# Query products and their sums for four positions in one buffer, V products for two, logits as position, offset, head

## The chip, the cores and the metric

The kernel runs on one core of a Trainium2 chip. The metric is device time in microseconds (us) of one execution. Five engines work side by side, each on its own queue in order: PE (TensorE, matmuls), DVE (VectorE), ACT (ScalarE), POOL (GpSimd) and SP (SyncE, which here only issues DMAs). ACT and POOL issue DMAs too.

## The reference

Two mixers over the same input x (2048 positions, 640 columns) and a gate between them. A is a local attention: 32 heads of 20 columns, each position looks at 8 keys, those 0, 2, ..., 14 positions back. B is a filter in the frequency domain.

```
qkv = (x @ wqkv).reshape(B, S, 3, H, Dh)          # H = 32, Dh = 20
idx = pos[:, None] - 2 * arange(8)[None, :]        # 8 offsets, masked where negative
logits = einsum("bhsd,bhswd->bhsw", q, kg) * Dh ** -0.5
attn = softmax(logits, -1)
o = einsum("bhsw,bhswd->bhsd", attn, vg)
a = o @ wo
b = irfft2(rfft2(x) * (w_r + 1j * w_i))
g = sigmoid((x * gate_w).sum(-1, keepdims=True))
out = g * a + (1 - g) * b
```

## The kernel before

Position 16 p + j lies in partition p as row j, so a partition holds 16 neighbouring positions; even and odd j never meet in the attention and are worked on apart (`par` 0 and 1, 8 rows each). The work falls into stages on PE: `qkv` (x times wqkv as three matmuls of rounded parts; the results leave through ACT into a DRAM scratch), `freq` (16 groups g, each a small pipeline over PE, ACT, POOL and DVE: `u`, `v` on PE, `ab` on DVE, `x`, `z` on PE, `P` on POOL, `s` on DVE, `g` on PE) together with `project_even` (attention output of even rows times wo), `spatial` (the inverse transform over columns) and `project_odd`.

The attention itself uses no matmul. `attend` does it for one `par` and a group h of four heads (80 columns); there are 16 such calls, called units here and named 0a, 0b, 1a, ... 7b. A unit loads q, k and v rows from the scratch. Then, for pairs of positions jj, it multiplies q with the eight k rows (product `pr`) and sums it over the 20 columns of each head into the logits `L` (a `TENSOR_REDUCE` on DVE). Both are 1280 elements a partition long. DVE makes the product with q copied to PSUM (`qbank`) by ACT; in ten of the units (table `POOL_PR`) the last pair's product is POOL's, straight from SBUF. After the masks (ACT) come the largest logit per position and head `m` (DVE), the subtraction (POOL), the exponential (ACT), the sum `s` and its reciprocal (DVE), the scaling (POOL), and for each pair the V products `pv` (POOL, one instruction for each position) and their sum over the offsets, `o` (DVE).

The order on every engine is fixed: `Plan.record` writes each operation into a list, `Plan.order` permutes the list by a table of numbers (`ORDER`), and `Plan.issue` issues it in that order. All instructions therefore carry one line (L385 in the profile), and are told apart by their tiles.

Of the kernel before, what the change touches and what calls it, by code (L numbers as in the profile page):

```python
# [208 lines left out]
HQ(%xOkCb5Ti|9M&74oX@)~%FC+g&Um>cIj7Th&a$THElCM_Qxh94S8@_R$YuH^AlZ29A62|gtX_GwKt861v*&%|Lj%A~%)Ju4ard*J9-%@(h(=zcz=9{hy8`{2ylZ=~+70?!1ipBf(&
zwb}8-f;L(FVHcuzwYP7?2%s*U{nv&ECs$KBfw^t@z;C&Xf&zSgn_WXO0Ra-A{p=`KSTo&WCxLcHX{frWWSucqtk!hm#2nHJeX5P<a5rX;@Kti_Yl8ko7HnBP?BD0BCR!|nSp+9pO(On  # L210
7C*Q$o$wOs&SmSBdiC|DHG?D8$uS*E_ccd=5LY{i^BiXwbd{r0)D57<l%^E2DaY|53+8~ZxRJddAoRNdJYPz%5Lvh5W}S={Qu`$OJ}cwneg)RxR)(xpZMXtIs%DRMvJ7u?%%!@^1B8h@
(qlVz@tLYv`rnaOHo>WRfe{k*SBQiEnDF!z+o6MsFAJ=(MehAC+OQk;gfj{$D4Y9E8C&GfcpM}t1W|C%hJ#;L!7aan3ZqicP~xB7_Qnrj(tTe<@R?W&V{($jS4EF-5t#TOP0?OuT|3Qa
eIT(hT>jCQrecqER6AALUaUC?)=4v!RW)w9%$6TmkX}rmdZ1<A!<Ce0_LGFT-55A$ndz>!p$dHdxh1>o=3<(6z*KuxX86ZbhMDSB?~D@~6mK>u#>!XP<ORCokbE-Ovd^FevYd6|yTLNh
6LqbJKy?z;o)=#fxd)}q(t!E7s4(3|QOszQKMHHgt&?pyfYSMq-!@LPp=HMQOrhAsZ-JWy-C3Mc^Z`{5!$bngKocKj*>1lOfpe>gL<4DAk0)0!w_E-I8Ix5zA0pAPHAB79wZiA}lY^=h
Std;TST@mvK(Izv+y2xl{ZkLjAJfK%G&=WMvx-dxg6DMA424jO9cS?4TWJptst&`UzGq$ZfJ_rYlV4K31$NLXrgHytE*H`DST?S8Z+_yEBRpdjK2A~uXM4Nj32C4N!P4z2;Hqn$;QEkU
x#r;cod7g-0_+HHSjTx0G?wMOQFZ}koI>bLqzm3R1#oY}9`o)-A1NE;d6CRy2FU=-R;2owOP)Xp5@L{{lo`pBpk%V|R6g=MDVwD`bNH=OjT}S9%<^i$H2}^WSgi-blEMMxNCWOt@KVe#
HqSpv<!^C>%lNmv7RSF7$EOxNC{yKe#`U(Lx+?J!T>!ZP9DRYha-KfY6f?D)z+1)BTY#H0H8P_on~L7A?2-f-TVGlJ$NYiPg`Ivs?eZmoz*1s%9Xd;!3V#C-+$0Brl2%!N#H_A1i{L@S
P#-7P*l5}1Q+W5C%(=qlbU3pZ%otQHBXliSa7Eq92vyz1<`-h2wlnrTN(?T$K{1wyGNT3yESJ?d;(Zw=a_uas{jBg++Q~Nj2jh-_=z=SgoGX(xs<sgT2K8=TN&l`u^j-}yWbYSO(5cEw
hVcGl#lx!tpndKnI3W6}4nYMD+Pk`P27A{L32W`ao5f1Lx*Nb1X()n(JDUZ2O2az;7O<uub@cq%>A*E(_tL!Qq_R=1wNX@G<vau7PJDCp_$;h81hHJ;PIGy_$BYC9!FRj&Q%d@dloNT&
V}(@XS$iJK7_UBeT9exaHe0ZCd>(H!PSGFR8O~kQ=y2V-@rw&$Jg2mnKHs;xrCurTIvRujMxI%zzSsUAbNQyk@KBwL05WxN*Sm)5I2Xq^XZjzH)Ihl#)t51ss6A^!b?3)adQa(X1?V`Q  # L220
wEf(@vgv8sXd>1A(Inx$aDsF9o|pp|HZf+o&w(aEY-(nPPdJX2mvN>(E_fL#$UQPvI|Oa9cnbzr-e$^;-WQD_g83Pq)JF@6puq4=iw_oAzI4h0IpY+hbO=V@zz#KK7T>Y)df*No_7zw#
J`ZNS1m5yd>sTzrvwN&$9|njAQz>w>cl%q7wQZn?8p!=9m>5`9rRfIf_1}m*K9QWX2p$bk-U|1B1Z(^)NFjGTUi*=`v=?z{hl`I|qiO|ofbK~N2V}%VS*t!h=6?gk(z$O~7sEFHmYj%6
MNgL}676SI+-J!42{U}iie@2JyD7wX?tWyweu6+;9xiJSQlECBlw3cU6JNL9Qbq$0tUe_bx^QVlnRQ^tl#ei^!;Uy@((9<|ywE43$z4IgNR)3HBAWp^wA5G)i`pF3l<h}x3OgiJc*rTp
yDIhR4d;b1#P9;B=Fn!{JagvZWQ8Dna+>C8?PWN5+e!O%eKQFD7&UwCI9EJuzf24eM=px5vm)*=iSJQOsoOrV0(&B;X_MREg42C+90%XRnO_)k_RRKzcw`jk&FlJtxyJ@dT+yf~v((s8
-2h}>WX&Km>`JDrIZsB~HyMCyj)w7Emh<Bxtc+@vJ<-~GPXyd<K2@BwUFJSEEbOSLf-}5Tj30C4oH>gKhj@`yM0lgO1I|~8Uz5d)n(Ap~u7*R$VC*4V^uL@BrFYVSXJ!#;GPx$-`iB^*
2MiYfr5xOz@(Hn_ZO=uraJXL7TjCH2Oo22&4b<5GbESU)fMy@w<%JD=kBRvs^7YntD5lPeG0~#A(Y7f~=u1vSN3y;*%B)if3ZHyCNgsIjl_GRnl%27NSP+9t2PA;2H4bS5GyaV=>j*#x
*M~~EY1!7%?esLp+*GX}o-QD6C&^J6=;H8X|6(A(`yZi}Z}faaS0?Gjqv@lj&ep&tv$=yAF_CROwlnc;Gg~`p{^9llwa}e7zb`&fYr`LIz+M4&!D;pBW0~8c-9pQAVK~5|Lst>X_XHJf
BbHYtz@n{+NemE;D#YqvNyi@TUL%=x!c}A)W#~0YXI_9y%G_JmIy7up9F-wz0Ko(;nI?_m?Kd3a(}245c2v@Jf1OP32?$)b@4&S%LtI4Xl7SDnL8i5%lEDj)>G1TqOFDWr8uzjy&O3Nm
d$+wYoEer$Aq-KST1DqGF`N6nbu3i9J1y!73cVHXcW7RCc*0zmf=AnkP~}&rJ5)<G5jD!ivtsQGa!*YrUZ<x(O%YP2uxAQgki#<4cU6)m;~U+_$c%HUxDD2C>6*du+*nLhT21G%FSMTx
F9o90(I?=4__Uh>X7zl2S;|3%g?xk&&ZNy<yz%i{Sl87#;Hq(*dX#-S;0K7k`-=_DNmtn_cWizA<)OfVpjTP3DV~JDA&$35ndX-;RJ~3efGwiJ5Ht%!mBpiuzqzwAm%V<N$YT+%N<y?-  # L230
L$<-n`T;@{9ha=_DU5Caogirb*l5ll(=hVGvPaUVHGn@TTk@(O%Cg>+!F&Z>^a}MWs*HoAIXZ*IGmD&KQ1$s5UlW<f%b`0L6Zo}XxY*ejMiL6wZB3VWksk25LDcc$*m+|kO*MiA5qM!R
E4&I$iUB%e=t-&vI#oE3omS`8qhKNa{&xtjquCoj@gt~4hPP`#R?lah{_Fr2NG)2)6j`)6xWw-bn!#53kreFmg|f%8{Hi9hP;wz{AL5rvcI#V0DymT1c(Kucy<*0`8=s--Bri8zDH~#v
%-FB#M0Qq%ICg_IFP2C48|n56Sm9Um9k2fiPvpqah%)KEUW1~=uV*6=QB*z{Al8lvW9Q;ye=6Tp=v>L79H5IQ5X|z~#8hpnJr+Ga_QrkC4`Rhv7#WXovCK>ybSs8B6l~NOoIP)O5Fr!S
+}fcYgLx<p#v>wbK=gW?vhdCXZVtgKhsHNHj%~Qolp5+lQ(hjj51#p5_1_2~j|^=(cHJD!9j9&qpZdcxvk%!cXv8;;W{9m%oyJFbB38c|mac656_T8#{}Kg@00
# [732 lines left out]
```

## Time and profile before

| | |
|---|---|
| time, median of 3 runs | 453.96 us (453.48 to 454.35) |
| the profiled execution | 455.89 us, of which the span from the first to the last instruction is 454.1 us |
| PE busy | 441.2 us, 97% of the span |
| PE weight loads | 391.8 us, 86% |
| DVE busy | 409.8 us, 90% |
| POOL busy | 363.9 us, 80% |
| ACT busy | 211.9 us, 47% |

How to read it: PE is busy nearly all the time, so the time can only fall by what PE waits, and it rises when PE is made to wait more. DVE and POOL are second; where they stand still matters only if PE, or the end, waits for them. Busy times are unions, and the durations of neighbouring instructions on one engine overlap a little, so what an instruction costs a full engine is the distance from its start to the next one's.

### The profile page before, as it was taken

The page shows a single profiled execution, that of the slowest core. Times are in us where ns is not written, and L with a number is a line of the kernel's source. Part 1 is how long each engine was busy: PE and PEld are TensorE (multiplying, and loading weights), DVE is VectorE, ACT ScalarE, POOL GpSimd, SP SyncE. Part 2 cuts the span into 40 slices and gives each one's busy share as a digit, 9 for nine tenths or more (in the row PEclk, how much of TensorE's full clock was granted, in tenths as well). Part 3 has the DMA queues.
Part 4 walks back from the last instruction along what each step waited for, and adds up shares of the span by engine and source line. Part 5 has one row for each costly group of instructions (what it writes and reads, how often), then busy time and mean ns, then how long its engine had stood idle before and what let it go on. Part 6 is the DMA issues. An engine that isn't in the chain of part 4 may idle for free. (4 is left out here: it accounts for less than half of the span.)

```text
span 454.1 us, 7249 instructions
## 1 busy us (share of the span) xinstructions
PE 441.2 (97%) x2440; PEld 391.8 (86%) x2440; DVE 409.8 (90%) x519; ACT 211.9 (47%) x561; POOL 363.9 (80%) x316
## 2 busy tenths in 40 slices
PE   9999999999999999999998989999989999999996
PEld 6888888888889888899886769998877899999996
DVE  4899999899999999999978989999999997899484
ACT  4723165625226463255356666667554655342110
POOL 1158895899899898988977898976899998889810
PEclk9999999999999999999998999999999999999999
DMA  8998999887968979679979778989883331365932
GB/s 312 401 383 268 340 330 377 305 264 237 272 183 272 340 217 316 181 216 320 303 220 294 240 230 250 297 245 320 258 257 105 85 97 54 118 207 134 296 123 87
DMA packets 73956, 110.75 MB, mean 244 GB/s; under 512 B 21296, under 2 KB 50992, under 8 KB 73920
## 3 DMA queue, kind: packets, MB, share of 16 engines
q1 hardware_dynamic: 40192, 69.32, 46.8%
q10 hardware_dynamic: 32816, 36.97, 26.1%
q0 software_dynamic: 912, 4.00, 2.4%
q8 instruction: 19, 0.31, 0.3%
q14 instruction: 17, 0.14, 0.1%
HBM read 72.51 MB, written 32.84 MB: 232 GB/s over the span
## 5 line engine op out<-in xcount | busy, mean ns | idle before, releaser
L385 PE MATMUL qkv<-w,xo 128*128 128x480 f32 (+1 forms) x480 | 110.6, 385 | 0.0
L385 PE MATMUL qkv<-w,xe 128*128 128x480 f32 (+1 forms) x474 | 104.3, 382 | 0.0
L385 PEld LDWEIGHTS qkv<-w,xe 128*128 128x128 f32 x474 | 89.3, 189 | 15.2 <-ACT xe L385 0.9
L385 PEld LDWEIGHTS qkv<-w,xo 128*128 128x128 f32 x480 | 89.7, 189 | 13.8 <-ACT zg L385 0.2
L385 ACT COPY ev<-qkv 128x480 f32<-128x480 f32 x64 | 34.9, 558 | 48.3 <-PE qkv L385 35.9
L385 PE MATMUL woa<-wo,oT 128*128 128x320 f32 x240 | 47.2, 318 | 0.4 <-ACT oT L385 0.4
L385 PE MATMUL wob<-wo,oT 128*128 128x320 f32 x240 | 46.9, 315 | 0.2 <-ACT ya L385 0.2
L385 POOL TENSOR_TENSOR P<-P,wp 128x963 f32<-128x963 f32 (+1 forms) x16 | 35.4, 2212 | 6.6 <-DMA P<-X 4.0
L385 PEld LDWEIGHTS woa<-wo,oT 128*128 128x128 f32 x240 | 37.7, 188 | 1.1 <-ACT oT L385 0.6
L385 PEld LDWEIGHTS wob<-wo,oT 128*128 128x128 f32 x240 | 37.8, 188 | 0.6 <-ACT ya L385 0.4
L385 POOL TENSOR_TENSOR fx<-fx 128x160 f32<-128x160 f32 (+1 forms) x16 | 12.8, 818 | 24.2 <-DMA fc<-in_t_fc 17.1
L385 POOL TENSOR_TENSOR w<-raw,w 128x480 fp32r<-128x480 f32 (+1 forms) x20 | 24.8, 1262 | 5.3 <-ACT w L385 5.3
L385 ACT CAST oT<-oTp 128x384 fp32r<-128x384 f32 (+1 forms) x32 | 13.4, 427 | 30.9 <-PE oTp L385 17.3
L385 PEld LDWEIGHTS g<-mm,s 128*128 128x128 f32 x150 | 21.0, 190 | 7.1 <-ACT zg L385 5.0
L385 PE MATMUL g<-mm,s 128*128 128x128 f32 x150 | 23.5, 280 | 3.1 <-ACT zg L385 3.0
L385 DVE TENSOR_TENSOR oT<-oTp,oT 128x384 fp32r<-128x384 f32 (+1 forms) x32 | 15.2, 485 | 11.0 <-ACT oT L385 10.7
L385 PE MATMUL oa<-gt,zg 128*128 128x161 f32 (+1 forms) x96 | 24.0, 344 | 0.0
L385 PE MATMUL ob<-gt,zg 128*128 128x161 f32 (+1 forms) x96 | 22.0, 344 | 0.0
L385 PE MATMUL u<-bt,zc 128*128 128x240 f32 (+2 forms) x96 | 21.1, 335 | 0.7 <-DVE ab L385 0.7
L385 PE MATMUL v<-bt,zc 128*128 128x240 f32 (+2 forms) x96 | 21.5, 335 | 0.2
L385 DVE TENSOR_TENSOR fx<-fx 128x642 f32<-128x642 f32 (+2 forms) x24 | 19.2, 798 | 0.7
L385 PEld LDWEIGHTS u<-bt,zc 128*128 128x128 f32 x96 | 16.9, 199 | 2.9 <-PE g L385 0.9
(304 smaller groups left out, 1107.6 us busy)
## 6 DMA issues: line engine op xcount, KB each, us to landing
qkvd<-ev ACTq DMA_DIRECT2D x32, 480.0 KB, 4.8
wp<-in_ws SPq DMA_DIRECT2D x16, 642.0 KB, 5.9
raw<-in_wqkv SPq DMA_DIRECT2D x25, 240.0 KB, 5.9
fx<-in_x SPq DMA_DIRECT2D x8, 641.0 KB, 7.9
ot<-od SPq DMA_DIRECT2D x16, 320.0 KB, 3.9
P<-X ACTq DMA_DIRECT2D x30, 160.5 KB, 4.6
fd<-fx POOLq DMA_DIRECT2D x6, 640.0 KB, 5.6
f<-fd SPq DMA_DIRECT2D x6, 640.0 KB, 6.1
```

The costliest lines, as they stand in the source:

```text
L385: p.dve.memset(w, 0.0)
```

## The change

In `attend`, with `POOL_PR` as it was:

- The q copy, the product and its sum are made for four positions at once (2560 elements) where DVE makes them all, and for two where the last pair is POOL's. Of 54 products and 64 sums on DVE 32 and 42 are left, which is 22 fewer of each (the first four positions in all 16 units, the last four in the six units without a POOL product). The two `pr` buffers for two positions become one for four; the three places of `qbank` become one for four and one for two positions.
- The V products of two positions are one instruction: 64 instead of 128.
- The logits lie as position, offset, head (8, 8, 4) where they lay as position, head, offset (8, 4, 8). The sum of products now writes them without gaps. `m` and `s`, which reduce over the offsets, now read with a step of four elements (16 bytes) and took their eight offsets side by side before. The masks are written for the new layout.
- `ORDER` is a new table.

```diff
 ORDER = """
-T>t<81poj4|NsC0{{R31`zHT%QmDPk&^9H>y=H*?`Lk%9Gnl%)B_CdQV7rLsIrdLM6sJFoVB8Rk|2U=URH5DLwHy3}>N|I2375U5sNENOZ_r>p;QjNS0Qt^d&3_BFn1BL!{U(U9<aW#`
+T>t<81poj4|NsC0{{R31`zHT%QmDPk=#MDKuavHX(-*4-BtL4lZ(KsIOtW*vbH(DXn{6x>Y7x4d+OGq=Ut3x;+j-bV#DI*Cv$$xAC(TD;868c`#R9Own^O!b`yiAzYmH!y&eRc)d7yAj
...
-        self.qthird = [qb[:, GC * i : GC * i + GC] for i in range(3)]
-        self.qturn = -1
+        self.qplace = qb[:, 0 : 2 * GC], qb[:, 2 * GC : 3 * GC]
...
-        L = self.Lr.next(f"L{nm}", 8, 4, 8)
-        for jj in range(0, 8, 2):
-            pr = self.prr.next(f"pr{nm}{jj}", 2, 8, HC)
+        L = self.Lr.next(f"L{nm}", 8, 8, 4)
+        own = POOL_PR.get((par, h), ())
+        jj = 0
+        while jj < 8:
+            k = 2 if jj in own or jj % 4 or jj + 2 in own else 4
+            if jj % 4 == 0:
+                pair = self.one(f"pr{nm}{jj}", 4, 8, HC, tag="pr")
+            pr = pair[:, jj % 4 : jj % 4 + k]
             w = kt[:, jj : jj + 8]
-            w = bass.AP(tensor=w.tensor, offset=w.offset, ap=[w.ap[0], [HC, 2], [HC, 8], [1, HC]])
-            if jj in POOL_PR.get((par, h), ()):
-                mul, qj = G.tensor_mul, q[:, jj : jj + 2]
+            w = bass.AP(tensor=w.tensor, offset=w.offset, ap=[w.ap[0], [HC, k], [HC, 8], [1, HC]])
+            if jj in own:
+                mul, qj = G.tensor_mul, q[:, jj : jj + k]
             else:
-                self.qturn = (self.qturn + 1) % 3
-                mul, qj = V.tensor_mul, self.qthird[self.qturn]
-                A.copy(qj, q[:, jj : jj + 2].rearrange("p j c -> p (j c)"))
-                qj = qj.rearrange("p (j c) -> p j c", j=2)
-            mul(pr, w, qj.unsqueeze(2).broadcast_to([128, 2, 8, HC]))
+                mul, qj = V.tensor_mul, self.qplace[k == 2]
+                A.copy(qj, q[:, jj : jj + k].rearrange("p j c -> p (j c)"))
+                qj = qj.rearrange("p (j c) -> p j c", j=k)
+            mul(pr, w, qj.unsqueeze(2).broadcast_to([128, k, 8, HC]))
             V.tensor_reduce(
-                out=L[:, jj : jj + 2].rearrange("p j h r -> p j r h"),
+                out=L[:, jj : jj + k],
                 in_=pr.rearrange("p j r (h d) -> p j r h d", d=HD),
                 axis=AX.X,
                 op=ALU.add,
             )
+            jj += k
...
-        V.tensor_reduce(out=m, in_=L, axis=AX.X, op=ALU.max)
-        G.tensor_sub(L, L, m.unsqueeze(3).broadcast_to([128, 8, 4, 8]))
+        V.tensor_reduce(out=m, in_=L.rearrange("p j r h -> p j h r"), axis=AX.X, op=ALU.max)
+        G.tensor_sub(L, L, m.unsqueeze(2).broadcast_to([128, 8, 8, 4]))
         A.activation(out=L, in_=L, func=AF.Exp, scale=SCALE)
         s = self.sr.next(f"s{nm}", 8, 4)
-        V.tensor_reduce(out=s, in_=L, axis=AX.X, op=ALU.add)
+        V.tensor_reduce(out=s, in_=L.rearrange("p j r h -> p j h r"), axis=AX.X, op=ALU.add)
         V.reciprocal(s, s)
-        G.tensor_mul(L, L, s.unsqueeze(3).broadcast_to([128, 8, 4, 8]))
+        G.tensor_mul(L, L, s.unsqueeze(2).broadcast_to([128, 8, 8, 4]))
...
-            for i in range(2):
-                G.tensor_mul(
-                    pv[:, i].rearrange("p (h d) r -> p r h d", d=HD),
-                    vt[:, jj + i : jj + i + 8].rearrange("p r (h d) -> p r h d", d=HD),
-                    L[:, jj + i].rearrange("p h r -> p r h").unsqueeze(3).broadcast_to([128, 8, 4, HD]),
-                )
+            w = vt[:, jj : jj + 8]
+            w = bass.AP(tensor=w.tensor, offset=w.offset, ap=[w.ap[0], [HC, 2], [HC, 8], [1, HC]])
+            G.tensor_mul(
+                pv.rearrange("p j c r -> p j r c"),
+                w,
+                L[:, jj : jj + 2].rearrange("p j r h -> p (j r) h").unsqueeze(3).broadcast_to([128, 16, 4, HD]),
+            )
```

What the new table does is seen on the engines. DVE, where the attention begins (unit 0a: products, sums, then `m0a`), before:

```order
L385 TENSOR_TENSOR pr0a_344<-kt0a,qbank 128x1280
L385 TENSOR_REDUCE L0a<-pr0a_344 128x2x8x4
L385 TENSOR_TENSOR pr0a_345<-kt0a,qbank 128x1280
L385 TENSOR_REDUCE L0a<-pr0a_345 128x2x8x4
L385 TENSOR_TENSOR pr0a_346<-kt0a,qbank 128x1280
L385 TENSOR_REDUCE L0a<-pr0a_346 128x2x8x4
L385 TENSOR_TENSOR pr0a_347<-kt0a,qbank 128x1280
L385 TENSOR_REDUCE L0a<-pr0a_347 128x2x8x4
```

and after the change:

```order
L382 TENSOR_TENSOR pr0a_344<-kt0a,qbank 128x2560
L382 TENSOR_REDUCE L0a<-pr0a_344 128x128
L382 TENSOR_TENSOR pr0a_345<-kt0a,qbank 128x2560
L382 TENSOR_REDUCE L0a<-pr0a_345 128x128
L382 TENSOR_TENSOR pr0b_358<-kt0b,qbank 128x2560
L382 TENSOR_REDUCE L0b<-pr0b_358 128x128
L382 TENSOR_REDUCE m0a<-L0a 128x32
```

Eight instructions became four of twice the size, and `m0a` stands behind one long product and sum of the next unit, where it stood behind two short ones of each.

DVE, where the attention meets the first groups of `freq` (`ab1` and `ab2` are what PE needs for groups 1 and 2), before:

```order
L385 TENSOR_REDUCE o7a0_478<-pv7a0_479 128x160
L385 TENSOR_TENSOR pr6a0_504<-kt6a_500,qbank_63 128x1280
L385 TENSOR_REDUCE m7b_492<-L7b_487 128x32
L385 TENSOR_TENSOR ab1_606<-u1_605,vs1_604 128x321 x2
L385 TENSOR_REDUCE L6a_503<-pr6a0_504 128x2x8x4
L385 TENSOR_TENSOR pr6a4_506<-kt6a_500,qbank_63 128x1280
L385 TENSOR_REDUCE L6a_503<-pr6a6_507 128x2x8x4
L385 TENSOR_REDUCE o7a0_478<-pv7a2_480 128x160
L385 TENSOR_REDUCE L6a_503<-pr6a4_506 128x2x8x4
L385 TENSOR_TENSOR ab2_616<-u2_615,vs2_614 128x321 x2
```

and after:

```order
L382 TENSOR_TENSOR pr6a0_484<-kt6a_480,qbank_63 128x2560
L382 TENSOR_REDUCE o7a0_460<-pv7a0_461 128x160
L382 TENSOR_REDUCE L6a_483<-pr6a0_484 128x128
L382 TENSOR_TENSOR pr6a4_485<-kt6a_480,qbank_63 128x1280
L382 TENSOR_REDUCE m7b_472<-L7b_469 128x32
L382 TENSOR_TENSOR ab1_574<-u1_573,vs1_572 128x321 x2
L382 TENSOR_REDUCE o7a0_460<-pv7a2_462 128x160
L382 TENSOR_REDUCE L6a_483<-pr6a4_485 128x64 x2
L382 TENSOR_TENSOR pr6b0_498<-kt6b_494,qbank_63 128x2560
L382 TENSOR_TENSOR z1_577<-z1_577,wp1_569 128x321
L382 TENSOR_TENSOR ab2_584<-u2_583,vs2_582 128x321
```

One sum of 1280 elements (half of `L6a` from `pr6a0`) and the product `pr6a4` moved ahead of `ab1`; the long product of the next unit, `pr6b0`, moved ahead of `ab2`.

POOL, late in `freq` (`P13`, `P14` are products of the groups 13 and 14 that DVE, and then PE, wait for; `pv6b` are V products), before:

```order
L385 TENSOR_TENSOR pv6b2_528<-vt6b_517,L6b_519 128x8x80
L385 TENSOR_TENSOR P13_781<-P13_781,wp13_772 128x963
L385 TENSOR_TENSOR P13_781<-P13_781 128x321
L385 TENSOR_TENSOR pv6b2_528<-vt6b_517,L6b_519 128x8x80
L385 TENSOR_TENSOR pr5b6_555<-kt5b_548,q5b_550 128x1280
L385 TENSOR_TENSOR P14_794<-P14_794,wp14_785 128x963
```

and after:

```order
L382 TENSOR_TENSOR pv6b2_504<-vt6b_495,L6b_497 128x2x8x80
L382 TENSOR_TENSOR P13_749<-P13_749,wp13_740 128x963
L382 TENSOR_TENSOR P13_749<-P13_749 128x321
L382 TENSOR_TENSOR pr5b4_527<-kt5b_522,q5b_524 128x1280
L382 TENSOR_TENSOR P14_762<-P14_762,wp14_753 128x963
```

The two halves of a V product that stood on both sides of `P13` now stand ahead of it as one (`pr5b4` is the POOL half of the unit's second buffer, the product called `pr5b6` before).

More of the change, by code (lines that the diff above doesn't have):

```diff
@@ L209 @@
[L209 to L228, printed above, removed]
@@ L233 @@
-%-FB#M0Qq%ICg_IFP2C48|n56Sm9Um9k2fiPvpqah%)KEUW1~=uV*6=QB*z{Al8lvW9Q;ye=6Tp=v>L79H5IQ5X|z~#8hpnJr+Ga_QrkC4`Rhv7#WXovCK>ybSs8B6l~NOoIP)O5Fr!S
-+}fcYgLx<p#v>wbK=gW?vhdCXZVtgKhsHNHj%~Qolp5+lQ(hjj51#p5_1_2~j|^=(cHJD!9j9&qpZdcxvk%!cXv8;;W{9m%oyJFbB38c|mac656_T8#{}Kg@00
+T>t<81poj4|NsC0{{R31`zHT%QmDPk=#MDKuavHX(-*4-BtL4lZ(KsIOtW*vbH(DXn{6x>Y7x4d+OGq=Ut3x;+j-bV#DI*Cv$$xAC(TD;868c`#R9Own^O!b`yiAzYmH!y&eRc)d7yAj
+EI>SOMgyW|6IVlz?{etRp_rXb`FX*NuqcMI^kM|llCB(6G53>*B7=3~M0{u0Ya=^0f(PmqZ`fHQAq`b>c)G-m!{1GMkeO%3w5!`|y?wx@|1ewjdT@=Kl@C5@x#p3D<QH;VZ}5?8U3pvb
@@ new lines @@
+h@<J-B|+HRrQKW%$FZarh$91qAkyv5{G#RdK}ro(AV36-B_h$#Rl)Rw7bsS21{Xg{+35i~^m;jS5l$I}9A(gM<s8!?|5o47Y?^P*(xHMdCQ?Rgw~gB-vGf)t`k{C7Ja}(v?b`#_Fm7P2
+t@}HpL*34cKwpbI<F1*YmaRvz%o2B)WHSXDM1g~?Z*~dMYB-mKX@T+H35mNyq%3#OT-kd&;V-%KI|-SkW}c)8+0PjmVuu*~Y&yCqpvp7m;WM-vk@G%4V1=Qqo9h~~3Jny1*LkU~9jZM)
+=u%rc=2lu`#GwqxQivx`Pe6oMyJ=>B>C7=kMKJ@!Y$jlrcizcKL(7dW@Se-U2tr{}zjg>c`H_|Z%Ut-p-kX_6g!?Ab4J`u;qVDyW=>1PJ*{rafynC-e@b{l6<%URB3tab}Zj&eH-3$H)
+;Cl%1;!l937-H%NjIN${UMHH<>m&j!@gQHkW_l~r?5w^T1L*?bACdldu^QdNM52Gau2Bz#V?o{cP33@E@2apO{lAl14wbe=m<%+6VWwMd03=emuOc|U=?=1=V9L)^?G9ZK`IAA6@A+ua
@@ new lines @@
++~U2nZO;W(H1ZH(CGu-wUc#xcD`O3qce|Ncy-#_qFJ_U_U6zKk)eCzi7%+;Fw|l~7Kors>22p6bS1HPYux`|h6J{7F0?UokWVlCTUbujk&wcgAh`KsGjwGyiOt-C&UQmi4C&S%FzT+IS
+1NEPmi0Os>c1!C;&y)GfMP1igl#4EVGuq<H2bEdO#j|e0GEUpu`s4uizn1)Upnb_kKieIGFo<{|f`ld;_4RJRFI(s!<UGOg0St5`6gfk?(9tzgFf%`3DWye-{FXy>tQvS#K}##qV3r{%
+<gs&=SqJznEK5JJv|OyfXaTG-Ha}^Zu>j0=KAZt0#S|S0LYPY*s<frPzlwl?s1Z`+Rn7vrX39zzNI)B`(1!3W?2-qpn@XY{mcLDe#W-T&6jeAxY6<H|WMl_`3@o0lFYFg!hBFEBT_6FE
+^IW|~W4Az943N&i7^h0C+)Aw}<cb@1RSi_&2{2A#$0W$*j6&C$TGle=iLeY0y++xEWc3|&q*OP4HK`NAyVim5$cczUieCIZV(|9x_0C<{>r|-5;GGUryt<eE@3thNEq(<#C<IfU+NA0d
@@ new lines @@
+Hd=3#DmwFuN>)9u;!ri)^61tufHct+60}DlD>MZ}*G{i^+{!oBAu}=PjrkGRp8P)lbN3{J#AgLczXbvHU5-$(-^ST3+NPQt@6uCe$`|)NA#`IwQ3!DeDCLGJ*+9MADA@d1eTkMN`&ND>
+H<+L1rxNppJ2-W~3xKCkmuJ-y`&a=;c%L)eI>6t``+XYR*r4&jO$>Oy<~JZs3#%G>Qp2q~RF6Z=Raz#uhgw8I0_P@Em|s}`H~{DnhsHWuC_F>HYIcQ2>bFOwZ@I1GS5?<C^1+uJU>laf
++~EOqoH@hs9~Z+wWY2liGWt0MSgI@Br2jxN#UcwHT%z@q^|@0C>$PQ=j?2*9aT^E1ETwI0TJX~s#u|(GBN2C#Ov)4im_Bk;no=6?3duB0v$CFD3eg}`ZXoh*DS|%JA_)Xj#cd3)zQ%8~
+ZR?N^Ob`5aTFu3WHTlZzD)mooY74i$E#SZ*_$;5fzUiHujdGV~J6oYhN%6nF4VzY-13VSA(uHQLBHy<P5*uVl){FxDs084k`+q}920T&hR&iwcuBogMJQa5YC7Uv5Qg(6M{|<V`R01Nt
@@ new lines @@
+bC;-rx##B)r?)R+sIwLqm)Q_^AYF;|K%in326~LLI}%THhds4{lJ4nX(uPMjbH-I>q+VBG#GfE=o4v!q$pAeZ#!V8L&+Vi7)Ya}Su;|)_;U5yK#HHRdD(+c#Wj)51f^{wQ|FB|~Wije(
+<XrS(8UbWb{YaV&opfTE0VGXO-#E30bEcoWWG+Fz#xvm$BfEt21R|nU*IS_@WmYblICb4v$>WJ-`9*DoBAt9#34OBC!+W(Yc_eZ&vwo_?fWiuV>XIB$EeK(-=*d)`cvC-W?Z>>&9(Hw&
+vcZ8X<fke13gcr{>^Pc+{0zhu?TzAO+PRz9<+Fv>FrM(M3&w_JPNnBtw<n`4kr9d<8RhxgO)tndSA0=`$0gcKCT^k65Hab8-1X7)pqZPG{J$sbF4G{gc|`USVyx=e!@{L!z-!`#ld)IS
+UV`q>zXSuEWiu<3FG&<!BT-c47dq?y8txA!vFQoOF@r6#b+zI5g4g+y1lbSrd|n2)x0S&)$-;%1z-K0WX01G8rL1OfQW4r3R^@;1c1fVWbfZE7--4i*tr_Nn5kzRx@lI^V&$xV2_}MMu
@@ new lines @@
+_v5J=qvOUM5OielQ`p6)(q=d!_$-s=x3K!9saUXUN)e1zmO4w^;Shf~yA1eIRcGs_U68Z%L`DM2MVx;N%*ThdRT0IdwtbgnLl0DAt2e4wv4%W8+WnOE&+qj0i&7<><;V#w879sb6CiFm
+hKWbI&5tn)u*vD%!;mN52+#QAUuU)iI<SRFpm*T|U#mqog4piRzP=*Fryc9V$F`fv72oc}Ku2dp>_wuos#&5RxD^xTz1+A_pB{vRM34Z@I9ZOu{l}y}1RdyZiU({Fq~UtA8t<!ctM9r2
+8^53URH7UX0iA)L-~$ipR}Cpof(%rB<&(;-Cfg6Jeni~-)Nk(WV3{Coh&H#Glrst)6xDpr$1|)&h#5j9tbMjcJBf^IC}zs|a;;UHCVgxsnOB!xw#cGa`c!MGEYAV^&mk+g%D(oVuGP&O
+5*v9(4L4tCNKGHYNTk`2$z*Y-59=3}+g!Dyd+$`ia<g&`_IYg56)~-sqBt)^cCYDK7;Ur#8!HjpJ0BkmjYpV!1}#upkuLvG-x9?~gQv7Au3Z}^Ao5DmdpcKD86E8v$LM(-CASj=1$3@n
@@ new lines @@
+65B1x3hVH8UO|@yO`SAcBM^G|X4Z`%g!02JrZN5~P)jm*_(8aLyeqE=SdxlseVG>(=sfuW8AZ7CjDj#Kup7>xS;E-=Nmamw!tpb8E#d*N_j3LGOo;Lq<1^gcZZyE;*+Wh5p08QqUXo<Z
+L9JcsE0pH+m4PpayFtp;-P$RG;%$XG{sTqDU3nSaY{RB3pke*2k@I6Eq~yqviEs#$PG`W6ets7<#iexFpPGiv7v}$mZzkvsgXk1JVX%?U?yoFU{F}ZawDuD4+i#5>&FeqE%7sH~LYNBk
+sTWm>jE`R@9E%)hokhCOlk|nmx66!sW|!yY=tBr}HwO3;g+*-b;J{dr=9D7BT1$>SWEcSJgv?;0EOGf$cRPCNnrMD4*Aj80YgL?+;1UgC$mdF&0>Wjcp45)y+6#`170~kDojXJ2lf42D
+)*-~k!L(WP(jUx0#k1T=mUBel=hr>(qJ!O9Kc1yv_I;c@A;f~1V5<B2h`I_9#mUSU;|T&E=L}rVSAuIyOUTeM!@lD7V}d<f2quD&)z=Z~O>I#=ZTN-&V?md)Q$FC+Dts^e5SfDNeIaG_
@@ L235 @@
+Y!p6+JE^cNFDbcKe)*;EXG*)YPd|~ZH5+YHqUNf$KJ*DM$F+);Tlw?0HrQQ0$j@4BimH`(8E?5hQ$0!sPB(tm#qMD~jtW<naQ*>{YY6~;&Z1V8NVc)M;AlAmZv5L@cLi9_kV4DB3D(Ny
+hKu6!CEGVRtnnv)_2E<blC|&ofM)fS{LvYA1^~pp<vfy*bYodx|MLSSHv
 """
@@ L294, in n @@
             return ring(*(f"{tag}{i}" for i in range(k)))
-        self.kvr, self.Lr, self.qr, self.prr = n("kv", 6), n("L", 3), n("q", 2), n("pr", 2)
+        self.kvr, self.Lr, self.qr = n("kv", 6), n("L", 3), n("q", 2)
         self.mr, self.sr, self.orr, self.pvr = n("m", 2), n("s", 2), n("o", 2), n("pv", 2)
@@ L578, in mask @@
         part = bass.AP(
-            tensor=ap.tensor, offset=ap.offset + first, ap=[ap.ap[0], [31 * step, n], [32, size], [8, 4], [1, size]]
+            tensor=ap.tensor, offset=ap.offset + 4 * first, ap=[ap.ap[0], [28 * step, n], [32, size], [1, 4], [4, size]]
         )
```

10 lines of the change are left out of this document (1 added, 9 removed).

## The prediction

> **What bounds the kernel now.** I read the head of the page first, then the busy time of the engines in stretches, then what PE waited for, then single stretches of DVE.
>
> ```profile
> span 454.1 us, 7249 instructions
> PE 441.2 (97%) x2440; PEld 391.8 (86%) x2440; DVE 409.8 (90%) x519; ACT 211.9 (47%) x561; POOL 363.9 (80%) x316
> ```
>
> PE is the bound on average, and the change adds or removes nothing on PE. So its worth lies in PE's waits alone. The stretches show where they are (columns: length, then busy us of PE, PEld, DVE, ACT, POOL with counts, the granted clock, DMA):
>
> ```profile
> 105.00:120.00 15.00, 15.00 (x71) 12.94 (x70) 15.00 (x13) 6.50 (x17) 14.82 (x12) 1.00 0.77 213
> 120.00:135.00 15.00, 15.00 (x71) 12.94 (x70) 14.96 (x15) 4.22 (x12) 13.99 (x11) 1.00 0.70 229
> 225.00:240.00 15.00, 14.31 (x71) 12.00 (x69) 12.30 (x12) 7.84 (x24) 12.04 (x11) 1.00 0.79 226
> 240.00:255.00 15.00, 12.81 (x60) 10.91 (x61) 13.17 (x23) 9.82 (x30) 12.17 (x11) 0.89 0.89 280
> 255.00:270.00 15.00, 13.05 (x75) 10.80 (x74) 13.31 (x21) 8.37 (x26) 13.00 (x12) 1.00 0.72 211
> 330.00:345.00 15.00, 13.62 (x88) 11.61 (x86) 14.35 (x22) 7.60 (x22) 14.43 (x10) 1.00 0.75 224
> 345.00:360.00 15.00, 13.97 (x85) 12.37 (x85) 15.00 (x15) 7.81 (x23) 14.92 (x13) 1.00 0.29 83
> 375.00:390.00 15.00, 15.00 (x96) 13.73 (x95) 12.01 (x22) 7.11 (x19) 12.10 (x11) 1.00 0.15 45
> ```
>
> While PE works on `qkv` it never stands still, and DVE is full too (15.00 and 14.96 of 15): the attention piles up behind DVE without costing anything yet. The bill comes at 225 to 270, where PE meets `freq`, whose `ab`, `z` and `s` stand in the same DVE queue behind the attention: PE loses 0.69, 2.19 and 1.95 us there, and again 1.38 and 1.03 us at 330 to 360, where DVE and POOL are full. After 360 DVE has air (12.01 of 15).
>
> ```profile
> PE g L385 <- ACT zg L385: 3.0, 5, 1.0
> PE x L385 <- DVE ab L385: 2.0, 1, 2.0
> PE z L385 <- DVE t L385: 1.2, 1, 1.2
> PE u L385 <- DVE ab L385: 0.7, 1, 0.7
> ```
>
> The longest single wait is for `ab2`, at 241.33. Ahead of it DVE had one long hole:
>
> ```profile
> 231.00 1.49 DVE L385 TENSOR_TENSOR pr6a<-kt6a,qbank 128x1280 f32<-128x1280 f32 x1 [2.56 <-ACT qbank L385]
> 240.70 0.88 DVE L385 TENSOR_TENSOR ab<-u,vs 128x321 f32<-128x321 f32 x2
> 241.33 0.78 PE L385 MATMUL x<-ab,mm 128*128 128x321 f32 x2 [2.02 <-DVE ab L385]
> ```
>
> So DVE's lateness at 240 reaches PE almost at once, less what the 2.56 us hole takes up. DVE's total is the number to work out.
>
> **Part 1: 44 DVE instructions fewer.** What a merge saves is the part of an instruction that doesn't grow with its size. Starts in the full stretch:
>
> ```profile
> 109.90 1.48 DVE L385 TENSOR_REDUCE o0b<-pv0b 128x160 f32<-128x1280 f32 x1
> 111.30 1.48 DVE L385 TENSOR_REDUCE L1b<-pr1b 128x64 f32<-128x1280 f32 x1
> 112.69 1.48 DVE L385 TENSOR_REDUCE o0b<-pv0b 128x160 f32<-128x1280 f32 x1
> 114.08 1.48 DVE L385 TENSOR_REDUCE L1b<-pr1b 128x64 f32<-128x1280 f32 x1
> 104.00 0.41 DVE L385 TENSOR_REDUCE m1a<-L1a 128x32 f32<-128x256 f32 x1
> 104.33 1.48 DVE L385 TENSOR_REDUCE o0a<-pv0a 128x160 f32<-128x1280 f32 x1
> ```
>
> They last 1.48 us but start 1.393 us apart; the one of 256 elements takes up 0.33 us. The line through both has 1.04 ns an element and 0.064 us fixed; 2560 elements then take 2.72 us where two took 2.79. 44 x 0.064 = 2.8 us less on DVE. The durations alone (1.48 and 0.41 us) would give 0.14 us fixed and 6.2 us; they overlap, so I don't take that. [...]
>
> **Part 2: `m` and `s` read with a step of 16 bytes.** There are 32, of 256 elements each. No DVE instruction in this trace reads so. The low end is the row of `m` above: the same work without a step, nothing added. The high end comes from rows in which DVE gets its float32 operands more slowly:
>
> ```profile
> L385 DVE TENSOR_TENSOR fx<-fx 128x320 f32<-128x320 f32 x8 | 6.5, 807 | 0.3
> 34.38 0.49 DVE L385 TENSOR_TENSOR fx<-fe 128x320 f32<-128x320 f32 x1
> ```
>
> The same size took 807 ns on average and 490 ns at best: 317 ns over 320 elements, 0.99 ns an element. There POOL worked on the same data, another cause, but it is the size of a halved supply. 256 x 0.99 = 0.254 us, x 32 = 8.1 us. Adding nothing and 8.1 us lie far apart. I take the high end: each element now lies away from the one before, and the DVE rows that depart most from 1.04 ns an element are these folds, which also leave the plain forward run.
>
> [...]
>
> Sum on DVE: from -2.8 to -2.8 + 8.1 = +5.3 us; taken, +5.3.
>
> **Part 3: what else moves.** The q copies go from 54 to 32, and ACT at 47% hides either:
>
> ```profile
> L385 ACT COPY qbank<-q1a 128x160 f32<-128x160 f32 x4 | 1.2, 299 | 2.3 <-DMA q1a<-qkvd 1.8 <-DVE pr0b L385 0.5
> L385 ACT COPY P<-x 128x321 f32<-128x321 f32 x16 | 7.0, 435 | 7.6 <-POOL P L385 3.7 <-PE x L385 2.2 <-DVE ab L385 1.4
> ```
>
> 299 ns each becomes about 435 for two, nothing on the path. But with one place for a four-position q, its copy can start only when the product before it is done. The sum between them (2.72 us) covers 0.44 us of copy unless ACT's queue stands at a PSUM copy; then DVE has a hole like the 2.56 us one, +0 to +2.5 us; I take 0, since a later DVE leaves ACT ahead.
>
> V products: one of two positions against two of one.
>
> ```profile
> L385 POOL TENSOR_TENSOR pv1b<-vt1b,L1b 128x640 f32<-128x640 f32 x8 | 10.8, 1447 | 0.7 <-DVE o1b L385 0.7
> L385 POOL TENSOR_TENSOR pr1b<-kt1b,q1b 128x1280 f32<-128x1280 f32 x1 | 3.0, 2997 | 0.0
> ```
>
> Two of 1447 are 2.89 us; POOL's 1280-element q product took 3.00. So 64 merges cost between a little less than nothing (a fixed part gone, at most some 0.06 us each as on DVE, -4 us) and 64 x 0.11 = +7 us of POOL. POOL has 15 - 13.99 = 1.0 us free in 120 to 135 and more at 225 to 270, and waits for DVE when DVE is late: nothing on the path. The instructions moved ahead of `ab1` (a sum and a product, 2 x 1.393 = 2.8 us) delay that one; after it the product `pr6b0` (2.72 us) stands ahead of `ab2` for them, so `ab2` is where it was, give or take 0.3 us. The masks, exponentials and subtractions keep their sizes.
>
> **Sum.** DVE is 5.3 us later from the middle of `freq` on (19 of the 32 reductions, 4.8 us, and 32 of the 44 savings, -2.0 us, come before `ab1`, where the moved 2.8 us make it 5.6). The hole of 2.56 us takes up its part, since what DVE waited for there doesn't come later. +5.3 - 2.6 = +2.7 us on PE; after 360 DVE's air hides the rest. The profiled execution took 455.89 us, so 458.6 for its like; it stands 1.93 above the median of 453.96, which gives 456.7 us.
>
> **Rivals.**
> A. The stepped read costs nothing. For it: the sums into `L` wrote with a 32-byte step before and took 1.48 us like `o`, which writes without one (though they write only once in 20 elements). Then DVE is 2.8 us earlier, and PE's waits for DVE in 240 to 270 (2.0 + 1.2 + 0.7) can shrink by it. I give it half, 1.5 us: 452.4, at most 451.2. It decides when a stepped reduction takes up under 0.33 + 2.8 / 32 = 0.42 us; above that DVE loses.
> B. Half the price (0.13 us each, 4.1 us): DVE +1.3, swallowed by the hole; 454.0, no change. The same comes if A's gain goes into coarser steps: `ab` waits for a 2.72 us instruction where it waited for 1.39.
> C. V products at the price of q products: POOL +7 us, more than its free time, PE then waits for `P`; with part 2 about 459.
> D. The table doesn't do what it did: holes such as that at 231.00 at other places, +2.5 us each on either side of the above; it widens the range.
>
> **How the numbers follow.** The forecast (most of the high price) has 0.46, A 0.35, B 0.13, C 0.06. Faster by over 0.2% (0.9 us, about what a measurement here can tell) are most of A: 0.31. Within: B's larger part and the rim of A and the forecast: 0.15. Slower: the rest, 0.54. The range goes from A's better half, 451.5, to the whole +5.3 with no hole to take it up, 459.3; the likeliest case's own is 455.0 to 459.3.
>
> **What would show it.** `m` and `s` at about 0.66 us each for 0.41; long products and sums starting 2.72 us apart; PE's wait for `ab2` near 5 us. I am wrong if `m` and `s` stay at 0.41 us, or if DVE is later and PE isn't, or if V products take over 3 us.

## The result, and the profile after

The changed kernel takes 458.11 us (median of 8 runs, 456.76 to 462.23), the kernel before 453.72 beside it: a ratio of 1.0101, 95% interval 1.0064 to 1.0138. It is slower by about 4.4 us, as forecast (456.7, range 451.5 to 459.3). The profiled execution took 458.24 us. Ratios, here and below, leave out slow runs (over 1.5% above the fastest of the same kernel) and compare each kernel with runs of the kernel before taken beside it (medians 453.66 to 454.72 us); one slow run of stepped_before, 461.57 us, counts in its median alone.

The head of the page, span and then busy time of the engines:

```profile
span 456.4 us, 7122 instructions
PE 440.5 (97%) x2440; PEld 390.1 (85%) x2440; DVE 413.8 (91%) x475; ACT 208.7 (46%) x539; POOL 358.2 (78%) x252
```

44 DVE instructions are gone and DVE is busy for 4.0 us longer (409.8 before). POOL lost 5.7 us. PE stands still for 15.9 us of the span (456.4 - 440.5), where it stood for 12.9. Stretches of the changed kernel, columns as in the prediction:

```profile
165.00:180.00 15.00, 14.45 (x85) 12.68 (x84) 15.00 (x12) 8.76 (x21) 12.76 (x8) 1.00 0.84 265
225.00:240.00 15.00, 14.61 (x74) 12.53 (x72) 14.88 (x12) 6.38 (x19) 14.18 (x10) 1.00 0.72 232
240.00:255.00 15.00, 12.59 (x71) 10.47 (x69) 12.85 (x23) 11.84 (x38) 10.98 (x10) 1.00 0.87 247
255.00:270.00 15.00, 12.56 (x71) 10.45 (x72) 12.76 (x18) 7.68 (x23) 13.05 (x10) 1.00 0.88 274
330.00:345.00 15.00, 13.82 (x89) 12.15 (x88) 13.80 (x21) 7.60 (x21) 11.13 (x7) 1.00 0.92 274
345.00:360.00 15.00, 12.73 (x76) 10.68 (x75) 13.25 (x13) 7.59 (x20) 14.84 (x9) 1.00 0.39 125
```

The hole of DVE at 225 to 240 is gone (14.88 busy for 12.30), and still PE loses as much at 240 to 270 (4.85 us for 4.14), more at 345 to 360 (2.27 for 1.03), and for the first time something inside `qkv`, at 165 to 180. The 4.14 us of before aren't quite comparable: its profiled execution had the granted clock at 0.89 on average from 240 to 255, and PE counts as busy for longer with the same work: the 128x161 matmuls of `u` and `v` took 475 ns each at 242.6 to 245.9, where half the clock was granted, and 300 ns at 270 to 330 (60 matmuls from 240 to 255, 71 after the change). What PE waited for:

```profile
PE g L382 <- DVE s L382: 3.3, 3, 1.5
PE u L382 <- DVE ab L382: 2.3, 4, 0.9
PE x L382 <- DVE ab L382: 1.6, 1, 1.6
PE g L382 <- ACT zg L382: 1.1, 3, 0.6
PE z L382 <- DVE s L382: 0.7, 2, 0.5
PE z L382 <- ACT ev L382: 0.5, 1, 0.5
```

The wait for `ab2` didn't grow, it shrank (1.6 us for 2.0). New are the waits for `s` (3.3 and 0.7 us), and those of `u` for `ab` grew (2.3 for 0.7); those for `zg` shrank (1.1 for 3.0). Around `ab2`, on DVE and then PE:

```profile
232.29 1.49 DVE L382 TENSOR_TENSOR pr6a<-kt6a,qbank 128x1280 f32<-128x1280 f32 x1
242.50 0.48 DVE L382 TENSOR_TENSOR ab<-u,vs 128x321 f32<-128x321 f32 x1
243.13 0.78 PE L382 MATMUL x<-ab,mm 128*128 128x321 f32 x2 [1.63 <-DVE ab L382]
```

The instructions whose prices the prediction guessed, on DVE by their starts:

```profile
103.60 0.61 DVE L382 TENSOR_REDUCE m1a<-L1a 128x32 f32<-128x256 f32 x1
104.12 1.48 DVE L382 TENSOR_REDUCE o0a<-pv0a 128x160 f32<-128x1280 f32 x1
105.52 2.81 DVE L382 TENSOR_REDUCE L1b<-pr1b 128x128 f32<-128x2560 f32 x1
108.25 1.48 DVE L382 TENSOR_REDUCE o0b<-pv0b 128x160 f32<-128x1280 f32 x1
```

and a V product of POOL, in the groups by shape:

```profile
L382 POOL TENSOR_TENSOR pv1b<-vt1b,L1b 128x1280 f32<-128x1280 f32 x4 | 10.7, 2725 | 1.5 <-DVE o1a L382 0.9 <-DVE o1b L382 0.6
```

`m1a` takes up 0.52 us to the next start where it took 0.33; the long sum takes 2.73. The V product of two positions lasts 2725 ns, two of 1447 were 2894.

### The profile page after: what moved, and what is told of

It is laid out like the page before. It is cut to its first block, busy times and chain, and to the rows that moved or that the text cites. A ratio compares the mean times of both kernels' runs of the same rounds, so it can differ in the third digit from the quotient of the medians.

```text
span 456.4 us, 7122 instructions
## 1 busy us (share of the span) xinstructions
PE 440.5 (97%) x2440; PEld 390.1 (85%) x2440; DVE 413.8 (91%) x475; ACT 208.7 (46%) x539; POOL 358.2 (78%) x252
## 5 line engine op out<-in xcount | busy, mean ns | idle before, releaser
L382 PE MATMUL woa<-wo,oT 128*128 128x320 f32 x240 | 48.7, 321 | 0.6 <-ACT oT L382 0.3
L382 PE MATMUL wob<-wo,oT 128*128 128x320 f32 x240 | 48.5, 319 | 0.2 <-ACT ya L382 0.2
L382 DVE TENSOR_TENSOR fx<-fx 128x642 f32<-128x642 f32 (+2 forms) x24 | 20.2, 841 | 0.6
```

Of the source, the lines that this page charges most:

```text
L382: p.dve.memset(w, 0.0)
```

## The experiments

Two theories to begin with. S: the stepped reads of `m` and `s` carry the loss. O: the order and the coarse instructions do.

| kernel | us | ratio to before, 95% interval |
|---|---|---|
| changed | 458.11 | 1.0101 (1.0064 to 1.0138) |
| plain_reads | 456.61 | 1.0060 (1.0037 to 1.0083) |
| stepped_before | 455.66 | 1.0026 (1.0001 to 1.0051) |
| merged_q_old_layout | 455.71 | 1.0038 (1.0013 to 1.0063) |
| step_prices | 455.0 | one run |
| new_table_nothing_merged | 458.35 | 1.0085 (1.0062 to 1.0108) |
| v_products_split | 458.51 | 1.0094 (1.0070 to 1.0118) |
| old_table_q_merged | 485.38 | 1.0696 (1.0672 to 1.0721) |
| changed_with_old_table | 488.37 | 1.0752 (1.0722 to 1.0783) |
| exchange_together | 459.0 | 1.0116 (1.0084 to 1.0148) |
| nothing_merged_three_mended | 456.85 | 1.0060 (1.0039 to 1.0081) |
| merged_old_layout_mended | 455.99 | 1.0052 (1.0032 to 1.0072) |
| old_table_pairs_together | 469.87 | 1.0341 (1.0310 to 1.0373) |

**The stepped reads, taken away and added.** plain_reads is the changed kernel in which `m` and `s` reduce eight neighbours (and the masks write 0, so that all stays finite); stepped_before the kernel before with the step of 16 bytes and masks of 0. Both reduce logits that don't belong together.

```diff
-V.tensor_reduce(out=m, in_=L.rearrange("p j r h -> p j h r"), ...)
+V.tensor_reduce(out=m, in_=L.rearrange("p j r h -> p (j r h)")
+                              .rearrange("p (j h r) -> p j h r", j=8, h=4), ...)
```

> The changed kernel with m and s reducing over neighbouring elements (all sizes, waits and the order as in the change). It leaves out the right softmax: the groups of eight that are reduced are not the offsets, and the masks write 0. Theory S (the stepped reads of m and s make the loss, 32 x 0.2 us on DVE): DVE busy falls by about 6.3 us from 413.8 to 407.5, m and s last 0.41 us, and the time goes to 452 to 454.5 us, level with the kernel before or under it. Rival O (the new order and the longer instructions make the loss): m and s get shorter too, but PE's waits stay where they are and the time stays at 457 to 459 us.

> The kernel before, with m and s reducing with a step of 16 bytes and nothing else changed. It leaves out the right softmax, as the groups reduced are not the offsets, and the masks write 0. Theory S: m and s last 0.61 us, DVE busy rises by 6.3 us from 409.8 to 416, and the time rises by what is left of that after a hole of 2.6 us, to 456.5 to 459 us. Rival O: the order is the old one, so the time stays at 453 to 455 us.

The reads are worth 5.9 us of DVE one way, 5.8 the other:

```profile
PE 439.7 (97%) x2440; PEld 390.2 (86%) x2440; DVE 407.9 (90%) x475; ACT 208.1 (46%) x539; POOL 358.0 (79%) x252
```

(plain_reads, 413.8 in the changed kernel) and

```profile
PE 439.5 (97%) x2440; PEld 390.0 (86%) x2440; DVE 415.6 (92%) x519; ACT 212.2 (47%) x561; POOL 365.0 (80%) x316
```

(stepped_before, 409.8 before). In time they are worth 0.41% and 0.26%, 1.9 and 1.2 us. Neither is far from the noise: the first is a difference of two ratios and uncertain by some 0.44% to either side, the second has 0.01% as its lower end. The rest of the 5.9 us doesn't reach the time; that it goes into air that DVE had is likely, not shown. Neither S nor O fits alone: without the step the changed kernel is still 0.6% slower.

**The price by step.** step_prices is the changed kernel with steps of 1, 2, 4 and 8 elements in `m` and 4, 16, 1 and 32 in `s` (its masks 0, its reductions of the wrong logits).

```diff
+b = (1, 2, 4, 8)[h % 4]    # for s: (4, 16, 1, 32)
+... in_=L.rearrange("p j r h -> p (j r h)").rearrange("p (a r b) -> p a b r", r=8, b=b)
```

> The changed kernel with m and s of the sixteen units reading with steps of 1, 2, 4, 8, 16 and 32 elements (4 to 128 bytes), 256 elements each; masks write 0 and the groups reduced are not the offsets, so the softmax is not the right one. Only the durations count. Theory S as a matter of the step: 0.41 us at 1 and 2 elements, 0.61 us at 4 and more. A rival: each doubling of the step costs more (0.41, 0.5, 0.61, 0.8). Another: only the 4-element step is slow by how it falls on the memory, and 8, 16 and 32 differ from it.

Groups by shape; the steps are, in this order, 1, 2, 4 and 8 elements in `m`, then 16 and 32 in `s`:

```profile
L382 DVE TENSOR_REDUCE m2a<-L2a 128x32 f32<-128x256 f32 x1 | 0.4, 414 | 0.0
L382 DVE TENSOR_REDUCE m2b<-L2b 128x32 f32<-128x256 f32 x1 | 0.4, 410 | 0.0
L382 DVE TENSOR_REDUCE m3a<-L3a 128x32 f32<-128x256 f32 x1 | 0.6, 608 | 0.0
L382 DVE TENSOR_REDUCE m3b<-L3b 128x32 f32<-128x256 f32 x1 | 0.6, 626 | 0.0
L382 DVE TENSOR_REDUCE s2b<-L2b 128x32 f32<-128x256 f32 x1 | 0.6, 601 | 0.0
L382 DVE TENSOR_REDUCE s3b<-L3b 128x32 f32<-128x256 f32 x1 | 0.6, 601 | 0.0
```

A step of 8 bytes cost nothing (410 ns for 414), one of 16 bytes 0.19 us for 256 elements (608 ns for 414), and from there to 128 bytes little or nothing was added (0.60 to 0.63 us in these rows; other units with a step of 32 bytes took 0.52 to 0.66). No run shows why the price comes between 8 and 16 bytes.

**Merging without the new layout.** merged_q_old_layout is the changed kernel with logits as before and each V product again two instructions, back to back.

```diff
-L = self.Lr.next(f"L{nm}", 8, 8, 4)
+L = self.Lr.next(f"L{nm}", 8, 4, 8)    # masks, m, s, V products as before
```

> The change without its new layout: logits as position, head, offset again, so m and s read side by side; products and sums for four positions and the new order stay; V products are two instructions for each pair again, one behind the other in the place of the one. Computes the reference. Theory S: DVE busy 409.8 - 2.8 = 407 us, POOL back at 364 us, time 451.5 to 454 us, faster than the kernel before by up to 0.5%. Rival O: new order and long instructions are still there, so 457 to 459 us. If POOL's merged V products were worth something on the path, this one is slower than the run with plain reads by that.

DVE has 1.6 us less work than before (408.2 us busy), reads nothing with a step, and the kernel is still 0.38% slower, between the two forecasts. So what is left is order or merging.

**Order or merging.** The next four cross the two tables with the two sets of instructions.

```diff
 # new_table_nothing_merged: before.py, every merged place of the new table
 # filled with the two instructions of before, back to back
-ORDER = <before>
+ORDER = <changed, expanded>
 # v_products_split: changed.py, per V product
-G.tensor_mul(pv, w, ...)          # two positions
+for i in range(2): G.tensor_mul(pv[:, i], ...)
```

> The kernel before in every instruction and size, with its three places for q, only put in the order of the changed kernel: where that has one merged instruction, here stand the two of before one behind the other. What remains of the loss once the stepped reads are gone (merged_q_old_layout, 0.4% over before) is either the new table's doing or the merging's. Theory T, the table: 456.5 to 459 us, over merged_q_old_layout, since DVE gets its 2.8 us of fixed parts back on top. Theory M, the coarse instructions and the single place for a four-position q: 453 to 455 us, like before, as neither is in this kernel.

> The changed kernel with each V product of two positions split into two of one, one behind the other at the same place of the order. POOL gets some 5.7 us more busy time and loses it where it waits. As I predicted (V products off the path): 457.3 to 458.9 us, as the changed kernel. The rival, that POOL's lateness reaches PE through P: 459.5 to 462 us; or, if the 2.6 us instruction holds up P more than two of 1.4 us do, 455 to 457 us.

> Merged products and sums and one place for q, but logits as before (position, head, offset), V products as before, and the order of before: a merged product stands where the first of its two stood, a merged sum where the second stood, and where the buffer isn't free by then, right behind. T: 451.5 to 454 us, as DVE has 2.8 us less to do and nothing else is new. M: 455 to 457 us, like merged_q_old_layout or more, since the coarse instructions and the one place are here too.

> The changed kernel with everything in it (layout, merged products, sums and V products), in the order of before. Its stepped reads cost 6 us of DVE, which cost 1.5 to 1.7 us of time in the two runs that took them away or added them alone. T: 453.5 to 455.5 us. M: 457 to 459 us, as the changed kernel.

No cost of the V products is seen: 1.0094 with two, 1.0101 with one. The new table costs 0.85% though nothing is merged in it, as T said. merged_q_old_layout differs from new_table_nothing_merged by the merging (and the q places) alone and is 0.47% lower, so merging does give some 2.1 us, for the 2.8 expected; with the intervals of both kernels that is 0.6 to 3.7 us. In new_table_nothing_merged most of the loss stands at the end of `freq`:

```profile
330.00:345.00 15.00, 12.79 (x82) 10.96 (x81) 13.09 (x18) 7.55 (x22) 11.69 (x8) 1.00 0.90 271
345.00:360.00 15.00, 13.00 (x67) 11.06 (x68) 13.32 (x16) 6.15 (x17) 14.92 (x12) 0.89 0.28 86
```

PE lost 2.4 us there before and loses 4.2 here (and 1.45 for 0.34 us at 270 to 330). DVE stands still too, for 1.9 and 1.7 us, and POOL for 3.3 us in the first of the two stretches; in the second POOL is full. So up to 345 no engine is full, which points to a chain of waits; what holds PE after that these lines don't tell.

The two kernels with merged instructions in the old table are 31 and 34 us slower, far outside both forecasts. In both some masks come ahead of a sum that they should follow, so part of the softmax is unmasked; what they show is the queue. ACT, in old_table_q_merged, waits for DVE to be done with the one place for q:

```profile
ACT qbank L387 <- DVE pr1a L387: 11.4, 2, 6.8
ACT qbank L387 <- DVE pr0b L387: 10.2, 2, 5.5
```

and the results of `qkv` and `g` stand behind it. How much of the 31 us comes of this wait wasn't measured: old_table_pairs_together below, with three places for q, already loses 15. In the changed kernel the same wait is there, smaller; its ACT queue at 165:

```profile
165.74 0.43 ACT L382 COPY qbank<-q3b 128x320 f32<-128x320 f32 x1 [2.79 <-DVE pr3a L382]
166.11 0.55 ACT L382 COPY ev<-qkv 128x480 f32<-128x480 f32 x1
...
169.29 0.54 ACT L382 COPY ev<-qkv 128x480 f32<-128x480 f32 x1
```

```profile
169.89 0.82 PE L382 MATMUL z<-fc,f 128*128 128x128 f32 x5 [0.55 <-ACT ev L382]
```

ACT holds 2.79 us for `pr3a`, the `ev` copies are late, and PE waits 0.55 us for the bank: the new loss of 165 to 180. With three places in the same table (new_table_nothing_merged) PE is busy for all 15.00 us of this stretch, with one place and the old layout (merged_q_old_layout) for 14.84.

**Three places of the new table.** In the new table the two DMAs that exchange the halves of `P14` are nine ACT instructions apart (none before), and POOL waits for it:

```profile
340.19 2.24 POOL L382 TENSOR_TENSOR P<-P,wp 128x963 f32<-128x963 f32 x1 [2.83 <-ACT P L382]
348.10 0.91 PE L382 MATMUL g<-mm,s 128*128 128x128 f32 x6 [1.53 <-DVE s L382]
```

Theory X: such places make the table's cost. Y: they only stand where another wait would.

```diff
 ACT dma_start P14 X14
+ACT dma_start P14 X14      # likewise P2, P11, P13
 ...                        # nine ACT instructions
-ACT dma_start P14 X14
 # the other two kernels also: pr6b0 from ahead of ab2 to behind it,
 # pr4a0 from ahead of s15 to behind it
```

> The changed kernel with one thing of its table mended: the two DMAs that exchange the halves of P are issued one behind the other again for P2, P11, P13 and P14, where the new table has 8, 7, 5 and 9 other ACT instructions between them. Theory X: these gaps are a large part of what the table costs, since POOL stands 2.8 us at 337 to 340 until P14 has landed, DVE then 1.2 us for P, and PE for s: 455.5 to 457 us. Rival Y: the wait for P only takes the place of another, since DVE is late at 330 to 345 anyway: 457.5 to 458.8 us, like the changed kernel.

> new_table_nothing_merged (458.35 us, 0.85% over before) with the exchanges together as in exchange_together and two pairs of products moved back behind small work that PE waits for: the pair pr6b0 from ahead of ab2 to behind it, the pair pr4a0 from ahead of s15 to behind it. X: these three places are most of what the table costs: 454 to 456 us. Y: the cost lies in many places or in the pairs' coarseness elsewhere: 457 to 459 us.

> merged_q_old_layout (455.71 us) with the same three places mended. DVE has 1.6 us less to do than before, no stepped reads, and none of the three waits. X: 451.5 to 453.5 us, faster than both kernels. Y: 454.5 to 456 us.

X was not borne out: all three kernels are slower than it said (nothing_merged_three_mended lies between X and Y). With the exchanges together the kernel isn't faster (1.0116). POOL's wait is gone for `P14` and stands before `P15`, in exchange_together:

```profile
335.36 2.25 POOL L388 TENSOR_TENSOR P<-P,wp 128x963 f32<-128x963 f32 x1
341.72 2.27 POOL L388 TENSOR_TENSOR P<-P,wp 128x963 f32<-128x963 f32 x1 [3.27 <-DMA P<-X]
345.48 0.91 PE L388 MATMUL g<-mm,s 128*128 128x128 f32 x6 [1.01 <-DVE s L388]
```

`P15`'s own exchange lands when it lands, and PE's last `g` waits 1.01 us for 1.53. This profile is of the fastest of the six runs: 455.81 us, the only one at the full clock; the other five, at 0.991 to 0.996, took 458.1 to 461.1. So what the mending gives at the full clock rests on one run and stays open. With all three places mended the unmerged kernel went from 1.0085 to 1.0060 (the intervals overlap), the merged one from 1.0038 to 1.0052. No version tried beats the kernel before.

**The grain in the old order.** The last kernel has before's instructions, places and table, but the two products that the change merges stand together, and so do the two sums. Some q copies and masks on ACT had to move with them.

```diff
-pr A, ..., L A, ..., pr B, ..., L B     # before, DVE
+pr A, pr B, ..., L A, L B               # old_table_pairs_together
```

> The kernel before, every instruction and its three places for q, in its own order, but for one thing: the two products that the change merges stand one behind the other at the first one's place, the two sums at the second one's place (moved one instruction further where a buffer isn't free), and the q copies and masks where these then allow it. This is the grain of the changed kernel, 2.8 us of one kind in DVE's queue where there were 1.4, without its table and without its merging. Theory G, the coarse grain itself is what the new order costs: 456.5 to 459 us, as new_table_nothing_merged. Theory T, the other moves of the new table do it: 453 to 455 us, like before.

3.4% slower, 15 us, with the same DVE work. Two long stretches of it:

```profile
45.00:135.00 90.00, 90.00 (x415) 77.71 (x414) 83.07 (x76) 35.75 (x91) 76.56 (x69) 1.00 0.85 279
240.00:360.00 120.00, 105.09 (x628) 91.99 (x627) 105.60 (x161) 70.45 (x198) 102.17 (x81) 0.97 0.78 243
```

the same two of the kernel before,

```profile
45.00:135.00 90.00, 90.00 (x415) 77.71 (x414) 86.47 (x78) 35.66 (x92) 79.45 (x71) 1.00 0.86 289
240.00:360.00 120.00, 113.11 (x687) 100.49 (x688) 112.81 (x168) 73.04 (x206) 104.98 (x81) 0.99 0.78 240
```

and the second of the changed kernel:

```profile
240.00:360.00 120.00, 110.58 (x677) 97.02 (x676) 109.15 (x154) 72.66 (x204) 99.18 (x63) 1.00 0.81 243
```

In these 90 us DVE gets 3.4 us less done than before and POOL 2.9, though PE is still full. What DVE of old_table_pairs_together waited for between 45 and 245:

```profile
DVE o0a L393 <- POOL pv0a L393: 2.2, 1, 2.2
DVE pr0b L393 <- ACT qbank L393: 1.8, 1, 1.8
DVE ab L393 <- ACT vs L393: 1.8, 1, 1.8
```

In the kernel before, DVE's waits there were for ACT's q copies (2.6, 1.3, 0.7 and 0.6 us) and one for a fold (0.9). DVE now stands for POOL's V products and for ACT too; that these in turn wait for the longer pairs is the likely reading, not one that these lines show. Most of the debt is paid at 240 to 360, where PE is busy for 105.1 us, 8.0 less than before. So the pairs are dear in an order made for halves, with what ACT had to move for them. The new table has the same pairs and loses only some 4 of the 15 us, so its other moves must give back about 11; which of them do wasn't separated, nor whether some of them cost. G said 456.5 to 459, T like before: G's direction, three times its size or more.

## Why the prediction was right, and where not

- *The sign and the time* (456.7 for 458.11) were right, the time in part by luck. The forecast's loss is the stepped reads less the savings and the hole, +2.7 us. Measured, stepped reads and merging about cancel (+1.2 to +1.9 and -2.1 us), and the slowdown comes from the new table, which the sum took at nothing.
- *Part 1, the fixed part.* Long instructions start 2.73 us apart, 2.72 was forecast. What merging gives in time, 2.1 us for 2.8, is the difference of two kernels under the new table, each with an interval 0.5% wide.
- *Part 2, the stepped reads.* The direction was right: `m1a` takes up 0.52 us where it took 0.33. The size was 0.19 us each for the 0.254 taken, 5.8 to 5.9 us of DVE for 8.1. DVE's sum is +4.0 us for +5.3. Rival B's half price (0.13) was off by as much on the other side. The rows that the 0.254 came from were read too simply. Of the eight folds behind the mean of 807 ns three took 493 ns, three 668 to 676, and two 1400 and 1561; in those two POOL was multiplying `w`, not working on the same data, and that DVE got its operands at half the rate there isn't shown by any run. That the high end came so near is luck.
- *The hole and `ab2`.* This step failed. The hole of 2.56 us did take up lateness (`pr6a` at 232.29 waits for nothing now), but the +2.7 us on `ab2`'s wait didn't come: 1.6 us for 2.0. What grew are the waits for `s` and those of `u` for `ab`; some two fifths of what PE lost more from 240 to 360 (1.0 of 2.5 us) stand at 330 to 360. The step treated DVE's lateness as one number that reaches PE at one place; the 5.8 to 5.9 us of DVE were worth 1.2 to 1.9 us of time.
- *Part 3, q's one place.* Taken as nothing, with a hole on DVE as the risk. The hole is on ACT: its copies wait for DVE, `ev` behind them is late, and PE stands at 169 (0.55 us). The kernel before had such waits of ACT too, up to 4.3 us long (until 137), and PE, busy throughout from 45 to 225, waited for none of them.
- *Part 3, V products.* Right as far as seen: no cost in the time, and at 2554 to 2858 ns under two of 1447.
- *Rivals.* A (a free step, 0.35) fell: 0.61 us. C fell. D, the table, had 2.5 us to either side for single holes, none of it in the sum, and is the largest term: +3.9 us (2.8 to 4.9) with nothing merged. What in the table costs stays open. The likeliest cause is what B named in passing, the coarser steps: by themselves in the old order they cost 15 us, and there DVE waits for ACT and POOL, not PE for `ab` alone. But the new table's other moves weren't tried without the pairs.

Together: table and grain +3.9, merging -2.1, stepped reads +1.2 to +1.9, V products 0. That is 3.0 to 3.7 of the 4.4 us; the terms come from different kernels and needn't add up.

## What to carry to other kernels

Merging two instructions saves a fixed part (here 0.06 us: a merged sum took up 2.73 us where two of 1.393 took 2.79) and doubles the grain at which everything behind them is served; ask first which queue holds on the merged one's buffers (here ACT, for 2.79 us on the one place for q), and try the pair back to back in the old order before writing the merged form. Price a new layout by all its readers: here a step of 8 bytes was free (410 ns for 414), one of 16 wasn't (608). And a wait that is mended at one place of a chain can show up at the next one (POOL's 2.83 us before `P14` became 3.27 before `P15`), so measure the time, not the wait.
